# 335 single moves in the planned engine queues of a two-layer attention and mixer kernel

## The chip, the cores and the metric

The kernel runs on one core of a Trainium2 chip. Such a core has five engines with a queue each: TensorE (PE in the profile; PEld is its weight load), VectorE (DVE), ScalarE (ACT), GpSimd (POOL) and SyncE (SP), which here issues DMA transfers. An engine works through its own queue strictly in the order in which it was written; engines wait for one another by semaphores. Matmul results land in eight PSUM banks, called b0 to b7 here. The metric is the time of one execution in microseconds (us); the time before is the median of three runs.

## The reference

Two layers, each an attention block and a mixer block, on x of 2048 rows (S) and 448 columns (D), 16 heads of 28 columns, F = 1792. The layer norms have no weights.

```python
def _A_ref(x, wqkv, wo):
    qkv = (x @ wqkv).reshape(B, S, 3, H, Dh)          # transposed to q, k, v by head
    scores = einsum("bhqd,bhkd->bhqk", q, k) * Dh ** -0.5
    p = softmax(scores, axis=-1)
    o = einsum("bhqk,bhkd->bhqd", p, v)
    return o.transpose(0, 2, 1, 3).reshape(B, S, D) @ wo

def _B_ref(x, w1, w2, w3, w4):
    h = gelu(layernorm(x) @ w1)
    # the four quarters of h's columns shifted by 1, -1, 2, -2 rows: g0 .. g3
    hs = concatenate([g0, g1, g2, g3], axis=-1) @ w2
    x1 = x + hs
    return x1 + gelu(layernorm(x1) @ w3) @ w4

x = x + _A_ref(layernorm(x));  x = x + _B_ref(layernorm(x))     # layer 1
x = x + _A_ref(layernorm(x));  x = x + _B_ref(layernorm(x))     # layer 2
```

## The kernel before, in words

All 16 heads of both layers' scores are cut into blocks of 128 keys by 512 queries (or the same number of elements in two key tiles by 256 queries). Four blocks, one for each head of a group, belong together, because a head has 28 columns and takes 32 of TensorE's 128 rows. The blocks form one stream through both layers. It is fed by the layer norm, the transposed normalized rows xT, and the projections to q, k and v; each finished chunk of rows passes on through wo and the mixer block while the stream runs on with other blocks.

*The exponentials.* ScalarE takes units of three blocks and of two blocks in turn (`unit_banks`, L1526): a wide unit in banks b0 to b2 (1536 columns) and a narrow one in b3 and b4 (1024 columns). `t_scores` (L1621) plans the score matmuls of a unit (`score_ops`, issued at L1500), `t_exp` (L1723) the exponential that reads them (L1738) and writes into PT, a ring of 15 slots; so unit u can't start before the PV matmuls of unit u − 6 have read their slots. As there are two sets of banks, the scores of the unit after next can only be written when an exponential has ended. Some blocks are kept from ScalarE: `d_first` (L1582) and the four steps of `d_chain` (L1609, L1611, L1613, L1616) compute them on VectorE with a polynomial.

*PV.* `t_pv` (L1750) plans probabilities times values: `mm` (L896) issues one matmul of 32 output rows per head, and the four heads of a group sit in the four column tiles of bank b5 and run together, as one round. At the end of a segment (a chunk of queries, a group of heads, a range of keys) `t_norm` (L1805) copies bank b5 out (L1819), and at a query chunk's end sends the denominators through rT (L1833, L1834) and rscr (L1836) and loads their broadcast into fb (L1841), all by DMAs on SP's queue; L1845 multiplies and writes otn.

*The rest of TensorE's work.* `mm4` (L898, issued at L905) splits a matmul of 128 output rows into the four column tiles. It serves the projections (wk_pad, wq_pad, wv), the statistics for q and k (sq with astat or astatq), wo (wo_pad with otn), w1 and w2, w3 (kT with w in the profile's names, because the transposed rows lie in a part of kT) and w4 (w with h2T). These go through banks b6 and b7. Evacuations on VectorE are L1252 and L1297 (k, q), L1326 (q), L1342 (v), L1902 (wo added to x_res), L2163 (w3) and L2201 (w4 added to x_res); L1238 squares q and k on POOL. Wide GELUs run on ScalarE over 7168 columns (L2185). The last chunk's groups are evacuated with the GELU itself, and its w4 goes out through `t_store` (L2213: L2216 on VectorE, L2220 on SP). Transposed rows come by a transposing DMA (`load_xT`, L1223, and `tr_dma`, L1115, both on SP) or by TensorE (`tr_pe`, L1118). `keep_pe_busy` (L403) puts filler matmuls on the identity (L2231) where TensorE would stand still for long.

*What sets the order.* Generators hand over operations; the list scheduler `Sched` (L275 on) runs them in planned time with planned durations and appends each operation to its engine's queue in `Plan` (L47 on). Nothing of this is decided on the chip. Each operation has a number, its position in the order of registration, over all engines. `Plan.add` (L160) finds the dependencies from what was registered before: the last writers of what is read, the last readers and writers of what is written. `finalize` (L194) makes semaphore waits of them and leaves out the waits already implied; `emit` (L245) writes each queue.

After the scheduler is done, `rearranged` (L120) may edit the queues. It takes operation a out of its engine's queue and puts it right behind operation b, for each pair (a, b) of `MOVES`, and then registers all operations again, in the order that `WEAVE` gives: one letter for each operation, t for TensorE, s for ScalarE, v for VectorE, g for GpSimd, d for SP, each taking the next operation of that engine's edited queue. Dependencies and waits are derived anew from this. If an operation would then read another writer's data, it raises an error.

```python
for (a, b) in moves:
    q = nxt[b]
    nxt[b], prv[a], nxt[a] = a, b, q
    if q is not None:
        prv[q] = a
```

In the kernel before both tables are empty (L19, L20) and `rearranged` isn't called (L2278).

Of the kernel before, what the change touches and what calls it, by code (L numbers as in the profile page):

```python
# [15 lines left out]
ENGS = ("pe", "act", "dve", "pool", "sp")  # L16


MOVES = ()  # L19
WEAVE = ()  # L20


class _Op:
# [646 lines left out]
def build_kernel(nc, A_x, A_wqkv, A_wo, B_x, B_w1, B_w2, B_w3, B_w4, out, n_layers=2):  # L670
# [85 lines left out]
    with st:  # L756
# [1520 lines left out]

        if WEAVE:  # L2278
            P = P.rearranged(MOVES, "".join(WEAVE))
        P.finalize(nc, st)  # L2280
# [55 lines left out]
```

## Time and profile before

| | before |
|---|---|
| median of 3 runs | 1029.74 us |
| lowest and highest | 1028.24, 1032.38 us |
| the profiled execution | 1028.64 us |
| its span | 1026.9 us |
| mean granted TensorE clock | 0.998 |

The profile is of one execution. Its span reaches from the first to the last recorded instruction; 1.74 us of the execution's time lie around it. "PT<-ps" names what an instruction writes and reads (buffer numbers left out), "128x1536" is partitions by elements, "x375" counts instructions. In square brackets stands how long the engine sat idle directly before, and what ended that. Records of neighbouring instructions on one engine can overlap, so short waits don't show as idle time. Rows of PE count its instructions; four matmuls of the four column tiles that run together count as four.

### The profile page before, as it was taken

The page shows a single profiled execution, that of the slowest core. Times are in us where ns is not written, and L with a number is a line of the kernel's source. Part 1 is how long each engine was busy: PE and PEld are TensorE (multiplying, and loading weights), DVE is VectorE, ACT ScalarE, POOL GpSimd, SP SyncE. Part 2 cuts the span into 40 slices and gives each one's busy share as a digit, 9 for nine tenths or more (in the row PEclk, how much of TensorE's full clock was granted, in tenths as well). Part 3 has the DMA queues.
Part 4 walks back from the last instruction along what each step waited for, and adds up shares of the span by engine and source line. Part 5 has one row for each costly group of instructions (what it writes and reads, how often), then busy time and mean ns, then how long its engine had stood idle before and what let it go on. Part 6 is the DMA issues. An engine that isn't in the chain of part 4 may idle for free.

```text
span 1026.9 us, 35814 instructions
## 1 busy us (share of the span) xinstructions
PE 973.9 (95%) x16107; PEld 410.4 (40%) x16109; DVE 809.6 (79%) x1572; ACT 983.0 (96%) x894; POOL 294.7 (29%) x462
## 2 busy tenths in 40 slices
PE   8999999999999999999999999999999999999998
PEld 3332444443333254343433443443434433444565
DVE  8876999999988958976867868697788588866651
ACT  7999999999999999999999999999999999999942
POOL 3312021430353006352435112012633130532230
PEclk9999999999999999999999999999999999999999
DMA  4633232220321013122241124424311020121101
GB/s 125 150 108 112 73 107 76 57 39 23 75 61 28 12 37 89 30 48 33 52 106 38 33 59 145 139 59 106 64 30 34 13 71 18 29 56 32 26 12 34
DMA packets 99393, 62.55 MB, mean 61 GB/s; under 512 B 68712, under 2 KB 88552, under 8 KB 99240
## 3 DMA queue, kind: packets, MB, share of 16 engines
q1 hardware_dynamic: 99240, 60.27, 23.3%
q8 instruction: 126, 2.06, 0.9%
q14 instruction: 27, 0.22, 0.1%
HBM read 28.16 MB, written 16.76 MB: 44 GB/s over the span
## 4 chain that ended last, share of the span: by engine, by line
ACT 67%; PE 28%; DVE 3%; DMA 1%; issue 1%; SPq 1%; DVEq 0%; ACTq 0%
ACT PT L1738 61%; PE ps L905 16%; PE ps L1500 6%; PE ps L896 5%; ACT h2T L2185 2%; ACT fb L2004 1%; DMA fb<-rscr 1%; ACT L2185 0%; DMA PT<-in_A_wqkv_dram 0%; DMA obf<-in_A_x_dram 0%; DVE yd L1582 0%; ACT sq L1235 0%; ACT hT L1986 0%; DVE PD L1616 0%; SPq L1223 0%
## 5 line engine op out<-in xcount | busy, mean ns | idle before, releaser
L1738 ACT ACTIVATE PT<-ps 128x1024 bf16<-128x1024 f32 (+1 forms) x782 | 887.7, 1318 | 5.8 <-PE ps L1500 3.6
L1500 PE MATMUL ps<-qT,kT 32*128 32x512 bf16 (+1 forms) x2304 | 270.1, 335 | 23.5 <-ACT PT L1738 17.3
L896 PE MATMUL ps<-PT,vaug 128*32 128x512 bf16 (+1 forms) x2420 | 247.2, 341 | 0.4
L905 PE MATMUL ps<-xT,w 128*32 128x512 bf16 (+3 forms) x2656 | 183.9, 344 | 4.3 <-DVE h2T L2163 2.4
L1500 PEld LDWEIGHTS ps<-qT,kT 32*128 32x128 bf16 x2304 | 69.9, 91 | 254.5 <-ACT PT L1738 222.0
L2231 PE MATMUL ps<-ident 128*32 128x256 bf16 x3348 | 146.0, 277 | 1.6 <-POOL ident L990 1.5
L896 PEld LDWEIGHTS ps<-PT,vaug 128*32 128x32 bf16 x2420 | 74.0, 95 | 89.6 <-issue 73.1
L2231 PEld LDWEIGHTS ps<-ident 128*32 128x32 bf16 x3348 | 95.4, 98 | 27.2 <-issue 11.6
L1845 POOL TENSOR_TENSOR otn<-ub,fb 128x512 bf16<-128x512 f32 (+1 forms) x31 | 36.6, 1180 | 208.7 <-DMA fb<-rscr 199.0
L905 PEld LDWEIGHTS ps<-xT,w 128*32 128x32 bf16 (+1 forms) x2656 | 70.0, 95 | 58.2 <-issue 26.7
L1582 DVE TENSOR_SCALAR yd<-ps 128x512 int32<-128x512 f32 x109 | 74.5, 685 | 19.1 <-PE ps L1500 18.3
L905 PE MATMUL ps<-w,h2T 128*32 128x448 bf16 x1120 | 76.8, 359 | 5.9 <-ACT h2T L2185 5.8
L1609 DVE SCALAR_TENSOR_TENSOR fb<-yd 128x512 f32<-128x512 uint16 x109 | 78.4, 724 | 0.5
L1611 DVE SCALAR_TENSOR_TENSOR fb<-fb,yd 128x512 f32<-128x512 f32 x109 | 77.2, 710 | 0.7
L1616 DVE SCALAR_TENSOR_TENSOR PD<-yd,PD 128x512 int16<-128x512 int16 x109 | 76.4, 702 | 1.6
L2163 DVE CAST h2T<-ps 128x512 bf16<-128x512 f32 (+1 forms) x70 | 44.5, 636 | 17.6 <-PE ps L905 16.5
L1238 POOL TENSOR_TENSOR sq<-qT 128x512 bf16<-128x512 bf16 x24 | 28.4, 1188 | 92.0 <-DVE qT L1297 89.1
L1238 POOL TENSOR_TENSOR sq<-kT 128x512 bf16<-128x512 bf16 (+2 forms) x32 | 30.3, 948 | 84.4 <-DVE kT L1252 81.3
L1613 DVE TENSOR_SCALAR PD<-fb 128x512 bf16<-128x512 f32 x109 | 49.7, 458 | 1.0
L905 PE MATMUL ps<-xT,wk_pad 128*32 128x512 bf16 (+2 forms) x576 | 47.7, 359 | 0.5 <-DVE vaug L1342 0.2
L905 PE MATMUL ps<-xT,wq_pad 128*32 128x512 bf16 x512 | 43.4, 382 | 0.6 <-issue 0.5
L905 PEld LDWEIGHTS ps<-w,h2T 128*32 128x32 bf16 x1120 | 30.3, 97 | 31.2 <-issue 10.2
(189 smaller groups left out, 1213.4 us busy)
## 6 DMA issues: line engine op xcount, KB each, us to landing
uscr<-ub SPq DMA_DIRECT2D x28, 256.0 KB
ub<-uscr SPq DMA_DIRECT2D x28, 256.0 KB, 7.0
fb<-rscr SPq DMA_DIRECT2D x24, 256.0 KB
xnd<-xn SPq DMA_DIRECT2D x28, 128.0 KB, 2.4
xd<-x_res SPq DMA_DIRECT2D x16, 224.0 KB, 2.2
x_res<-xd SPq DMA_DIRECT2D x16, 224.0 KB, 3.9
w<-in_B_w_dram SPq DMA_DIRECT2D x5, 448.0 KB, 7.5
obf<-in_A_x_dram SPq DMA_DIRECT2D x16, 112.0 KB
```

The source lines that it names most:

```text
L896: return lambda e: e.matmul(out=out, lhsT=lhsT, rhs=rhs, start=start, stop=stop, **kw)
L905: r.append(e.matmul(out=out[c:c + w, :], lhsT=lhsT[:, c:c + w], rhs=rhs, start=start, stop=stop, tile_position=(0, c)))
L1238: return both("sq", 0.15 + NW * 0.0018, 0.07 + NW * 0.00104, lambda e: e.tensor_tensor(out=sq[:, si, 0:NW], in0=src, in1=src, op=ALU.mult) ...
L1500: yield op("pe", (0.005 + NW * 0.00042) / nc_, lambda e, i=i, kc=kc, j=j, g=g, qt=qt, a=a, NW=NW, bank=bank: e.matmul(out=ps[:, bank, i * ...
L1582: yield op("dve", c_ps(512), lambda e: e.tensor_scalar(out=y, in0=ps[:, bi(bank), :], scalar1=SCALE * L2E * FS, scalar2=-126.0 * FS, op0=A ...
L1609: yield op(D_[0][0], D_[0][1], lambda e: e.scalar_tensor_tensor(out=q, in0=lo, scalar=E2 / E3 * FS, in1=lo, op0=ALU.add, op1=ALU.mult), re ...
L1611: yield op(D_[1][0], D_[1][1], lambda e: e.scalar_tensor_tensor(out=q, in0=q, scalar=E1 / E3 * FS * FS, in1=lo, op0=ALU.add, op1=ALU.mult) ...
L1613: yield op(D_[2][0], D_[2][1], lambda e: e.tensor_scalar(out=pdt, in0=q, scalar1=E3 / FS ** 3, scalar2=E0, op0=ALU.mult, op1=ALU.add), rea ...
L1616: yield op(D_[3][0], D_[3][1], lambda e: e.scalar_tensor_tensor(out=pdt.bitcast(I16), in0=hi, scalar=128.0, in1=pdt.bitcast(I16), op0=ALU. ...
L1738: yield op("act", 0.069 + n * w * 0.000833, lambda e, bk=bk, s0=s0, n=n, w=w: e.activation(out=PT[:, s0:s0 + n, 0:w], in_=ps[:, bk[0]:bk[0 ...
L2163: ev = op("dve", c_ps(m * NW), lambda e, hr=hr, pv=pv: e.tensor_copy(out=hr, in_=pv), reads=[("ps", bi(b))], writes=hk, touch=[b])
L2231: return [e.matmul(out=ps[32 * c:32 * c + 32, bi(b), 0:256].rearrange("p (a n) -> p a n", n=128), lhsT=ident[:, 32 * c:32 * c + 32], rhs=i ...
```

## The change

`MOVES` gets 335 pairs and `WEAVE` 104 strings of 11,186 letters in all. Nothing else in the source changes; every line below the tables stands 146 further down. By engine, 247 of the moved operations are TensorE's, 56 VectorE's, 17 GpSimd's, 9 SyncE's and 6 ScalarE's. 82 go to a later place, 253 to an earlier one or follow a moved neighbour (chains such as (564, 575), (565, 564) keep a group together behind its first). The letters come to 7914 t, 880 s, 1572 v, 458 g and 362 d, which is the number of operations of each engine before. None of the moves goes into the first 24 us of the profile; the last ones are in the stretch after the last exponential.

```diff
-MOVES = ()
-WEAVE = ()
+MOVES = (
+    (241, 247), (243, 241), (274, 285), (276, 274), (555, 550), (572, 568), (574, 572), (564, 575), (565, 564),
...
+    (759, 758), (856, 850), (857, 856), (858, 857), (930, 935), (931, 930), (937, 931), (966, 951), (975, 987),
...
+    (3339, 3343), (3787, 3779), (3788, 3787), (3900, 3883), (3901, 3900), (3891, 3895), (3917, 3933), (3919, 3917),
...
+    (5286, 5292), (5360, 5379), (5361, 5360), (5362, 5361), (5363, 5362), (5406, 5399), (5407, 5406), (5409, 5407),
+    (5410, 5409), (5457, 5491), (5746, 5683), (5700, 5717), (5701, 5700), (5745, 5739), (5820, 5836), (5822, 5820),
...
+    (9616, 9627), (9680, 9672), (9681, 9680), (9682, 9681), (9684, 9682), (9697, 9689), (9699, 9697), (9700, 9699),
...
+    (4904, 4882), (5515, 5505), (5488, 5515), (5593, 5607), (5678, 5657), (5912, 5878), (5951, 5905), (6131, 6120),
...
+    (1299, 1282), (4296, 4191), (4869, 4832), (7465, 7418), (7510, 7578), (8305, 8253), (11184, 11171),
+)
+WEAVE = (
+    "vdvvvvsgdvgvvdtgtvgdtvtgdtsgtgvdvtvttdvtvvtdttvtvdgtgtdvtvtdtstvvtdgsvtttdtsgtttttstttsvttttvstttttgtvttstttvt",
...
+)
```

Operations that the prediction names: 241 and 243 are the two scores of 24.14 us in the profile before; 3900 and 3901 the two w4 groups of 381.49, 3891 the wo group of 380.29; 756, 758 and 759 the three wv groups of 74.62; 5745 and 5746 the w4 group of 518.91 and the w3 group of 519.10; 9616 the first xT,w group of 887.06; 7465 the transposing load issued at 690.86; 5678 the addition (L2201) of 512.33.

101 lines of the change are left out of this document (added), and 34 rows, old and new, of the table MOVES.

## The prediction

> **What bounds the kernel now.** I read the page's busy shares first, then its chain by engine, then the stretch between the first and last exponential (exp) in the view of windows (after length and colon: busy us of PE, PEld, DVE, ACT and POOL, granted clock, DMA share, GB/s), the groups by shape, the chain in time, and at last the queues around each wait.
>
> ```profile
> span 1026.9 us, 35814 instructions
> PE 973.9 (95%) x16107; PEld 410.4 (40%) x16109; DVE 809.6 (79%) x1572; ACT 983.0 (96%) x894; POOL 294.7 (29%) x462
> ACT 67%; PE 28%; DVE 3%; DMA 1%; issue 1%; SPq 1%; DVEq 0%; ACTq 0%
> L1738 ACT ACTIVATE PT<-ps x782: 821/1277/1767, 16.2 to 971.9; 128x1536 bf16<-128x1536 f32 x190, 128x1024 bf16<-128x1024 f32 x6
> 16.21:972.90 956.69, 909.52 (x14715) 370.64 (x14719) 778.50 (x1482) 950.62 (x846) 281.18 (x424) 1.00 0.24 61
> L1738 ACT ACTIVATE PT<-ps 128x1536 bf16<-128x1536 f32 x375 | 577.0, 1539 | 5.7 <-PE ps L1500 3.6 <-PE ps L896 0.8
> L1738 ACT ACTIVATE PT<-ps 128x1024 bf16<-128x1024 f32 x406 | 447.8, 1115 | 0.1
> 114.05 89.09 ACT PT L1738 x79
> 999.42 23.83 PE ps L905 x532
> ```
>
> ScalarE is busy 950.62 of the 956.69 us from the first exp to the end of the last: 6.07 us of idle time shows. That understates the waits. The chain's unbroken run of 79 exps took 89.09 us, 2.255 us for a pair of a wide and a narrow one (39.5 pairs), while the records of such a pair last 1539 + 1115 = 2654 ns: neighbours overlap by 0.2 us each, and a wait shorter than that overlap isn't shown at all. By the spacing of the ends of all 782 exps against that cadence, the waits add up to about 10.7 us: four of 0.8 to 1.2 us, 17 of 0.15 to 0.5 us, the rest smaller. This is all that any order of the same work can win in this stretch, because the moves change neither the exps nor the GELUs. The 16.2 us ahead of it hold none of the moves. In the 55 us behind, the chain is matmul without a gap (532 in 23.83 us at its end), and the same matmuls are left.
>
> **The change part by part.** Of the 335 moves 247 are on PE, 56 on VectorE (DVE), 17 on GpSimd (POOL), 9 on SP and 6 on ScalarE. Every engine keeps its operations. The semaphore waits go from 4689 to 4665. So nothing is removed and nothing added; a move is worth what it takes off one of those waits. What comes directly ahead of 158 of the exps changes.
>
> *Rounds ahead of scores.*
>
> ```profile
> 24.14 0.39 PE L1500 MATMUL ps<-qT,kT 32*128 32x512 bf16 x2
> 24.45 0.81 PE L896 MATMUL ps<-PT,vaug 128*32 128x512 bf16 x8
> 24.90 3.71 ACT L1738 ACTIVATE PT<-ps 128x1536 bf16<-128x1536 f32 x3 [0.82 <-PE ps L896]
> 887.06 0.40 PE L905 MATMUL ps<-xT,w 128*32 128x512 bf16 x4 [1.21 <-issue]
> 887.27 0.49 PE L896 MATMUL ps<-PT,vaug 128*32 128x256 bf16 x9
> 887.51 0.90 PE L905 MATMUL ps<-xT,w 128*32 128x512 bf16 x12
> 888.34 0.39 PE L1500 MATMUL ps<-qT,kT 32*128 32x256 bf16 x6
> 888.78 6.88 ACT L1738 ACTIVATE PT<-ps 128x1536 bf16<-128x1536 f32 x6 [1.13 <-PE ps L1500]
> ```
>
> The exp at 24.90 waits for PV matmuls (L896) that free its PT slots. Two scores (moves 241 and 243) now go behind them: the PVs start at 24.14 in place of 24.45, a gain of 0.31. The scores come later by the first rounds, and are needed only when that wide exp is over, after 26.2. At 888.78 the exp waits for scores behind sixteen xT,w matmuls, and PE stands still for 1.21 us ahead of these. The nine PVs that ran among them are now put into that idle time. Four matmuls on the four column tiles run together as one round; by the tail's 532 in 23.83 us a round of 448 columns takes 0.179 us, so one of 256 columns 0.10. Nine PVs are three rounds: 0.31. The remaining 0.9 of this stall is the late xT and stays.
>
> *Filling holes in PE's queue.*
>
> ```profile
> 379.57 0.40 PE L896 MATMUL ps<-PT,vaug 128*32 128x256 bf16 x7
> 380.29 0.37 PE L905 MATMUL ps<-wo_pad,otn 128*32 128x448 bf16 x4 [0.32 <-DVE x_res L1902]
> 381.49 0.55 PE L905 MATMUL ps<-w,h2T 128*32 128x448 bf16 x8
> 73.89 0.37 PE L905 MATMUL ps<-wv,xT 128*32 128x448 bf16 x4
> 74.39 0.61 PE L896 MATMUL ps<-PT,vaug 128*32 128x512 bf16 x7
> 518.91 0.36 PE L905 MATMUL ps<-w,h2T 128*32 128x448 bf16 x4
> 519.10 0.28 PE L905 MATMUL ps<-kT,w 128*32 128x256 bf16 x4
> 519.21 0.38 PE L896 MATMUL ps<-PT,vaug 128*32 128x512 bf16 x1
> ```
>
> Two w4 groups (x8 at 381.49) go in among the PVs ahead of the 0.32 hole and no longer stand ahead of the next scores: up to 0.32; I take 0.30. The three wv groups behind the waiting PVs of 74.39 go ahead of them, into the gap 74.26 to 74.39: 0.13, taken as 0.15 for the shorter tail. The w3 group of 519.10 leaves its window and the w4 group of 518.91 goes one place up, so that the PV of 519.21, which waits for its block, needs nothing but its wait behind it: 0.11 (to 519.21) at least, up to 0.30, taken 0.20. About twenty smaller places of the same kind (a group less, or a hole filled, ahead of an exp with under 0.1 us to spare, each 0.05 to 0.24 by the same rounds of 0.10 or 0.18) come to 1.1. Where groups went, other windows get one or two rounds more; four of those have next to no slack: minus 0.4.
>
> *SP's queue.* Move 7465 takes the transposing load out of the way of a normalization.
>
> ```profile
> 690.86 2.69 SPq L1223 DMA_TRANSPOSE xT<-xnd  x1
> 693.59 0.55 SPq L1841 DMA_DIRECT2D fb<-rscr  x1
> 700.81 0.69 DVE L1845 TENSOR_TENSOR otn<-ub,fb 128x512 bf16<-128x512 f32 x1 [2.25 <-DMA fb<-rscr]
> 701.42 0.74 DVE L1297 TENSOR_SCALAR wk_pad<-ps,bc 128x512 bf16<-128x512 f32 x1
> 702.31 0.40 PE L905 MATMUL ps<-sq,astatq 128*32 128x512 bf16 x4 [0.94 <-DVE wk_pad L1297]
> 703.72 8.45 ACT L1738 ACTIVATE PT<-ps 128x1536 bf16<-128x1536 f32 x7 [0.66 <-PE ps L1500]
> ```
>
> The issue of 2.69 us stood ahead of the load of fb; VectorE waited 2.25 us for fb, its q evacuation behind was late, PE waited 0.94 for that, and the exp 0.66. With the transposes issued earlier, fb lands about 1.75 us earlier, still 0.5 us of VectorE's 2.25 remain, and PE's 0.94 is gone: the exp's 0.66 goes, and with what the overlap hides I take 0.70. The four DMA instructions of a normalization (L1833, L1836, L1802, L1841) keep their order among each other; the other eight SP moves go past weight loads that wait for nothing.
>
> *VectorE, POOL, ScalarE moves.* These 79 mostly bring an evacuation or a POOL product forward by one to three places. No row gives their price: above, it can't exceed the waits that PE's and SP's moves leave alone and that an evacuation could end (some 3 us, out of the rest of 10.7); below, there is the cost worked out under the VectorE rival. I take 0.9, near the lower middle, since most stalls rest on PE's order and only a few on an evacuation.
>
> *The tail.* Three w3 groups are postponed, transposes come earlier, and the last two banks swap their order. PE has no gap there to fill: 0.
>
> Sum: 0.31 + 0.31 + 0.30 + 0.15 + 0.20 + 1.1 − 0.4 + 0.70 + 0.9 = 3.6 us. The profiled execution took 1028.64 us (1.74 around its span of 1026.9); less 3.6, 1025.0. The runs' median, 1029.74, lies 1.1 above the profiled run; I leave that out of the centre and in the range. Half a per cent, what a measurement can tell from no change, is 5.1 us: faster means under 1024.6, slower over 1034.9, and the forecast sits on the first of these.
>
> **The throttle.**
>
> ```profile
> 903.21 2.25 PE L905 MATMUL ps<-w,h2T 128*32 128x448 bf16 x32 [1.96 <-ACT h2T L2185]
> 901.25:903.21 1.96, 0.00 (x1) 0.00 (x1) 0.00 (x0) 1.96 (x2) 0.72 (x1) 1.00 0.07 26
> 904.21:907.62 3.41, 3.41 (x44) 1.48 (x40) 0.78 (x3) 3.38 (x3) 0.00 (x0) 0.50 0.02 5
> 367.60:369.56 1.96, 0.00 (x1) 0.01 (x2) 0.00 (x0) 1.94 (x2) 0.00 (x0) 1.00 0.00 0
> 906.27 2.37 ACT L1738 ACTIVATE PT<-ps 128x1536 bf16<-128x1536 f32 x2
> 909.61 3.71 ACT L1738 ACTIVATE PT<-ps 128x1536 bf16<-128x1536 f32 x3 [0.97 <-PE ps L1500]
> ```
>
> After PE stood still 1.96 us for the wide GELU the granted clock was 0.50 for 3.41 us, and the exp at 909.61 came 0.97 late. The same 1.96 us at 367.60 were followed by no such stretch, so it depends on more than the gap. A PE that is packed more densely ahead of a GELU stands still longer before it; each such case costs about 1 us. I count none, and put it into the range.
> [...]
>
> **The rivals.**
> *More goes than I can place* (chance 0.22). Exps with little lead are released by chains that cross engines; moves for which I found no wait may each take a part of the 10.7 us. If the stalls not touched by name (0.97 at 909.61 and some 2 us of evacuation waits) are all that is left, 7.7 go: 1021. For it: 335 moves are spread over the whole stretch. Against: I found a wait behind about 30 only.
> *Waits reappear* (0.15). A stall that one exp loses comes back at the next, as when the xT transfer or fb is late by itself: then only 0 to 1 us is won and the kernel gives 1029. For it: the remaining 0.9 at 888.78. Against: an exp that starts earlier lets the next bank go earlier too, and no DMA but those two stands at a large wait.
> *VectorE held up by its own queue* (0.13, slower).
>
> ```profile
> 510.41 0.68 DVE L1611 SCALAR_TENSOR_TENSOR fb<-fb,yd 128x512 f32<-128x512 f32 x1
> 511.93 0.36 PE L905 MATMUL ps<-w,h2T 128*32 128x448 bf16 x2
> 512.33 0.62 DVE L2201 TENSOR_TENSOR x_res<-x_res,ps 128x448 f32<-128x448 f32 x1 [1.23 <-PE ps L905]
> ```
>
> Move 5678 puts the addition of 512.33 ahead of L1611 of 510.41, but its matmuls end at 512.29 (511.93 + 0.36): L1611 and the exp block done on VectorE behind it would start at 512.95, 2.5 us later. At seven more places an operation is put 0.4 to 1.4 us ahead of its input as the old order had it. If PE's moves don't bring these inputs forward, eight such delays of 1.8 us on average (mean of the waits 1.0 and the operation itself 0.6 to 0.7), of which 0.5 is covered, and all of it on the way to exps, make 8 × 1.3 = 10.4: 1028.64 − 3.6 + 10.4 = 1035.4. It decides where the blocks on VectorE have under 1.3 us to spare. Against: the operation behind is mostly a step of a block whose PV comes microseconds later, and PE's order was changed at those same places.
> That the change doesn't do what it says is excluded: the queues differ as the table has it, and each operation still reads the data of the same writers.
>
> **How the numbers follow.** Forecast 1025.0 at 0.50 (split by the edge 1024.6: 0.23 faster, 0.27 same); more 0.22, all faster; reappear 0.15, all same; VectorE 0.13, of which 0.11 over 1034.9. Faster 0.45, same 0.27 + 0.15 + 0.02 = 0.44, slower 0.11. The range goes from 1019 (the rival that wins more, with a spread of 2) to 1033 (reappearing waits, 1029, with the median's offset of 1.1 and three throttled stretches); the forecast's own is 1022 to 1028.
>
> **What would show it.** Right: the idle time before wide exps falls from 5.7 to about 3; the waits at 24.90, 382.42 and 703.72 are gone; the one at 888.78 shows 0.8 in place of 1.13; fb lands before VectorE has waited 1 us; the tail's length from the last exp to the end is the same. Wrong: exps that start on time now wait (new bracketed idles behind L1738), or VectorE shows waits of 1 us at L2201, L1902, L1819 with its blocks late, or several stretches of clock 0.50, or the stretch of exps shortens by more than 6 us, which would mean waits that the records hide.

## The result and the profile after

| | before | after |
|---|---|---|
| median of 17 runs each | 1028.24 us | 1025.12 us |
| lowest and highest | 1025.51, 1032.38 us | 1023.95, 1028.69 us |
| ratio of the runs | 1 | 0.9972, 95% interval 0.9961 to 0.9982 |
| the profiled execution, its span | 1028.64, 1026.9 us | 1025.07, 1023.4 us |

The medians lie 3.1 us apart; the forecast was 3.6 off the profiled execution, and 1025.0 us in all. The change is under half a per cent, which the prediction calls the same; it gave that 0.44 and faster 0.45. The page of the profile after, its windows from the first to the last exponential (exp) and its ScalarE groups by shape, as they were shown of before; all lines of the code stand 146 further down (L1738 is L1884):

```profile
span 1023.4 us, 35818 instructions
PE 969.9 (95%) x16109; PEld 408.7 (40%) x16109; DVE 813.1 (79%) x1572; ACT 981.0 (96%) x894; POOL 291.4 (28%) x462
15.96:969.55 953.59, 905.43 (x14708) 368.82 (x14710) 782.22 (x1482) 949.07 (x845) 277.94 (x424) 1.00 0.24 61
L1884 ACT ACTIVATE PT<-ps 128x1536 bf16<-128x1536 f32 x375 | 582.2, 1553 | 2.8 <-PE ps L1646 1.6 <-PE ps L1042 0.3
L1884 ACT ACTIVATE PT<-ps 128x1024 bf16<-128x1024 f32 x406 | 453.0, 1130 | 0.7 <-PE ps L1646 0.6
```

The last exp of before ended at 972.72, so its window of 956.69 us in the prediction reached 0.18 too far. The two spans differ by 3.57 us: 0.25 lie ahead of the first exp, where no move stands; 2.92 lie between the first and the last exp (956.50 and 953.58 us); 0.40 lie in the tail behind (54.20 and 53.80 us). The idle time ahead of wide exps fell from 5.7 to 2.8 us. The tail comes out at 53.8 in all five profiles that hold TensorE's moves and the others' together, at 54.4 with TensorE's alone and at 54.8 with the others' alone, so its 0.4 belongs to the order.

Where? An exp's end in the one trace less the end of the same exp in the other is a line with steps; each step is a wait won or lost at that exp. Here are the places that the prediction names and the largest that stay; pairs that cancel within three exps are left out (such as −0.52 at 420.40 and +0.52 at 423.96):

| exp of before at | step us | what stands there |
|---|---|---|
| 24.90 and the next | −0.51, +0.17 | moves 241, 243 |
| 75.94 | −0.18 | 756, 758, 759 |
| 268.59 | +0.63 | scores behind matmuls that wait for VectorE's x_res, which waits 0.84 us for a load of x |
| 382.42 | −0.31 | 3900, 3901, 3891, and VectorE's 3875 |
| 519.96 | under 0.1 | 5745, 5746 |
| 703.72 | −0.77 | 7465 |
| 755.47 | +0.88 | a tanh on ScalarE waits for VectorE |
| 867.09 | +0.81 | scores behind matmuls that wait for VectorE |
| 888.78 | −0.41 | 9616 |
| 909.61 | −1.08 | a stretch of half clock (0.50 for 3.41 us) in the profile before, none there after |

The timeline of ScalarE after, at five of these places (start, us, then what; in brackets the idle time before and what ended it):

```profile
24.14 3.88 ACT L1884 ACTIVATE PT<-ps 128x1536 bf16<-128x1536 f32 x3 [0.31 <-PE ps L1042]
378.83 6.98 ACT L1884 ACTIVATE PT<-ps 128x1536 bf16<-128x1536 f32 x6
697.88 9.40 ACT L1884 ACTIVATE PT<-ps 128x1024 bf16<-128x1024 f32 x8
887.03 6.88 ACT L1884 ACTIVATE PT<-ps 128x1536 bf16<-128x1536 f32 x6 [0.72 <-PE ps L1646]
904.51 3.71 ACT L1884 ACTIVATE PT<-ps 128x1536 bf16<-128x1536 f32 x3
```

At 24.14 the wait is 0.31 in place of 0.82, at 887.03 0.72 in place of 1.13; at 382.42 and 703.72 of before the exps now run on without one. The last row is the place of 909.61: no wait either. For 703.72, the queues of SyncE and VectorE after:

```profile
685.58 1.95 SPq L1369 DMA_TRANSPOSE xT<-xnd  x1
687.71 0.50 SPq L1982 DMA_DIRECT2D rscr<-rT  x1
690.21 0.56 SPq L1987 DMA_DIRECT2D fb<-rscr  x1
696.83 0.68 DVE L1991 TENSOR_TENSOR otn<-ub,fb 128x512 bf16<-128x512 f32 x1
```

The transposing load now stands ahead of rscr, in time that SyncE spent waiting for the reciprocals; fb is issued at 690.21 in place of 693.59, and VectorE's product doesn't wait.

The two large losses show on VectorE, whose rows here run past the two rows of GpSimd (POOL):

```profile
750.99 1.77 DVE L1755 SCALAR_TENSOR_TENSOR fb<-yd 128x512 f32<-128x512 uint16 x1
752.68 0.68 DVE L2149 SCALAR_TENSOR_TENSOR fb<-fb,hT 112x512 f32<-112x512 f32 x1
861.39 1.76 DVE L1757 SCALAR_TENSOR_TENSOR fb<-fb,yd 128x512 f32<-128x512 f32 x1
863.41 0.68 DVE L2309 CAST h2T<-ps 128x512 bf16<-128x512 f32 x1
...
750.91 1.30 POOL L1991 TENSOR_TENSOR otn<-ub,fb 128x512 bf16<-128x512 f32 x1 [8.38 <-DMA fb<-rscr]
861.32 1.29 POOL L1991 TENSOR_TENSOR otn<-ub,fb 128x512 bf16<-128x512 f32 x1 [24.22 <-DMA fb<-rscr]
...
753.39 0.63 ACT L2150 ACTIVATE fb<-fb 112x512 f32<-112x512 f32 x1 [0.77 <-DVE fb L2149]
864.14 0.40 PE L1051 MATMUL ps<-xT,w 128*32 128x512 bf16 x4 [0.80 <-DVE h2T L2309]
865.87 4.62 ACT L1884 ACTIVATE PT<-ps 128x1536 bf16<-128x1536 f32 x4 [0.71 <-PE ps L1646]
```

Two operations that mostly take 0.68 us took 1.77 and 1.76 us, each started within 0.1 us behind a GpSimd product of normalization (otn). What stands behind them on VectorE came 1.08 us late: the second step of a tanh GELU (L2149), for which ScalarE waited 0.77, and a w3 evacuation (L2309), for which TensorE waited 0.80 and the exp 0.71. In the prediction neither of these is a term. The trace before had the same kind of row, behind which no exp waited; the product beside it began at 150.34:

```profile
150.62 1.76 DVE L1609 SCALAR_TENSOR_TENSOR fb<-yd 128x512 f32<-128x512 uint16 x1
```

### The profile page after: what moved, and what is told of

Same layout as the page of the kernel before. It is cut to its first block, busy times and chain, and to the rows that moved or that the text cites. A ratio compares the mean times of both kernels' runs of the same rounds, so it can differ in the third digit from the quotient of the medians.

```text
span 1023.4 us, 35818 instructions
## 1 busy us (share of the span) xinstructions
PE 969.9 (95%) x16109; PEld 408.7 (40%) x16109; DVE 813.1 (79%) x1572; ACT 981.0 (96%) x894; POOL 291.4 (28%) x462
## 4 chain that ended last, share of the span: by engine, by line
ACT 71%; PE 23%; DVE 3%; DMA 1%; issue 1%; SPq 0%; DVEq 0%; ACTq 0%
ACT PT L1884 65%; PE ps L1051 13%; PE ps L1646 5%; PE ps L1042 4%; ACT h2T L2331 2%; ACT fb L2150 1%; PE ps L2377 1%; ACT L1884 1%; DVE h2T L2309 0%; ACT hT L2132 0%; DMA rT<-ub 0%; ACT L2331 0%; DMA PT<-in_A_wqkv_dram 0%; DMA obf<-in_A_x_dram 0%; DMA rscr<-rT 0%
## 5 line engine op out<-in xcount | busy, mean ns | idle before, releaser
L1884 ACT ACTIVATE PT<-ps 128x1024 bf16<-128x1024 f32 (+1 forms) x782 | 887.4, 1332 | 3.5 <-PE ps L1646 2.2
L1051 PE MATMUL ps<-xT,w 128*32 128x512 bf16 (+4 forms) x2656 | 178.1, 344 | 4.2 <-DVE h2T L2309 3.0
L1755 DVE SCALAR_TENSOR_TENSOR fb<-yd 128x512 f32<-128x512 uint16 x109 | 79.0, 728 | 0.7
L1757 DVE SCALAR_TENSOR_TENSOR fb<-fb,yd 128x512 f32<-128x512 f32 x109 | 78.3, 721 | 0.7
L2309 DVE CAST h2T<-ps 128x512 bf16<-128x512 f32 (+1 forms) x70 | 44.4, 635 | 16.0 <-PE ps L1051 14.9
L1646 PE MATMUL ps<-wk_pad,kT 32*128 32x512 bf16 x256 | 39.6, 384 | 4.5 <-ACT PT L1884 4.0
```

The lines of the kernel that those rows point to most:

```text
L1051: r.append(e.matmul(out=out[c:c + w, :], lhsT=lhsT[:, c:c + w], rhs=rhs, start=start, stop=stop, tile_position=(0, c)))
L1646: yield op("pe", (0.005 + NW * 0.00042) / nc_, lambda e, i=i, kc=kc, j=j, g=g, qt=qt, a=a, NW=NW, bank=bank: e.matmul(out=ps[:, bank, i * ...
L1755: yield op(D_[0][0], D_[0][1], lambda e: e.scalar_tensor_tensor(out=q, in0=lo, scalar=E2 / E3 * FS, in1=lo, op0=ALU.add, op1=ALU.mult), re ...
L1757: yield op(D_[1][0], D_[1][1], lambda e: e.scalar_tensor_tensor(out=q, in0=q, scalar=E1 / E3 * FS * FS, in1=lo, op0=ALU.add, op1=ALU.mult) ...
L1884: yield op("act", 0.069 + n * w * 0.000833, lambda e, bk=bk, s0=s0, n=n, w=w: e.activation(out=PT[:, s0:s0 + n, 0:w], in_=ps[:, bk[0]:bk[0 ...
L2309: ev = op("dve", c_ps(m * NW), lambda e, hr=hr, pv=pv: e.tensor_copy(out=hr, in_=pv), reads=[("ps", bi(b))], writes=hk, touch=[b])
```

## The experiments

Each kernel holds a part of the table `MOVES`; the letters of `WEAVE` register the edited queues again, by operation number as far as the data allow. The time of each stands beside runs of the kernel before on the same chip.

**No moves.**

```diff
-    (241, 247), (243, 241), (274, 285), (276, 274), (555, 550), (572, 568), (574, 572), (564, 575), (565, 564),
...
-    (1299, 1282), (4296, 4191), (4869, 4832), (7465, 7418), (7510, 7578), (8305, 8253), (11184, 11171),
```

> No moves at all; only the letters that register the old order again, so the queues and waits are those of the kernel before. Both theories expect the time of before (ratio 1.000, within 0.001). The profile is a second look at the same program: stalls that come from the order should come back in place and size (24.9: 0.93 end to end; 703.7: 0.77; 888.8: 1.24). Theory 'the 1.08 us that the changed kernel won at the exp of 909.61 is the throttle's luck': the half-clock stretch after the wide GELU near 903 is missing or elsewhere here in some looks. Rival 'the stall at 909.61 belongs to the old order': it is back with about 1.0 us.

1029.0 us, ratio 1.0008 (0.9996 to 1.002). The stalls of the order came back (no step of over 0.15 us at 24.9, 382.4 and 703.7). The one of 909.61 didn't: the exp there came 1.08 earlier than in the profile before. Other places were late instead:

```profile
369.47 4.52 PE L1009 MATMUL ps<-w,h2T 128*32 128x448 bf16 x56 [1.96 <-ACT h2T L2289]
370.10:373.50 3.40, 3.40 (x44) 1.59 (x40) 0.00 (x0) 2.98 (x3) 0.00 (x0) 0.50 0.17 63
374.36 2.37 ACT L1842 ACTIVATE PT<-ps 128x1536 bf16<-128x1536 f32 x2 [1.26 <-PE ps L1604]
```

The 56 matmuls behind the wide GELU took 2.83 us in the profile before and 4.52 here, at a granted clock of 0.50, and the exp came 1.37 late. Two more stretches of half clock stood near 108, where 0.45 and 0.17 were lost, and near 889, where 1.19 were. So the order before doesn't always lose the 1.08 of 909.61, and it isn't counted as a gain here. (Whether the change makes that loss rarer is taken up in the last section.)

That allows a cleaner comparison: each run lists its mean granted clock, and one stretch of half clock of 3.41 us lowers it by 0.0017 (half of 3.41 in some 1026). So, by this estimate, a run that lists 1.000 had none; the twelve profiled executions agree: 0.995 with three such stretches, 0.996 and 0.997 with two, 0.998 with one, 1.000 with none. Of the 72 runs of the kernel before beside the experiments 27 have a clock of 1.000.

| kernel | runs | mean of all | at clock 1.000: runs, mean |
|---|---|---|---|
| before | 72 | 1028.34 | 27, 1026.97 |
| the changed kernel (17 and 12 of its repeat) | 29 | 1025.62 | 10, 1024.58 |
| the twelve moves | 12 | 1025.67 | 6, 1024.79 |
| without 8107 and 9290 (three times) | 20 | 1024.81 | 6, 1023.38 |

At full clock the order is worth 2.4 us (1026.97 less 1024.58, with a standard error of 0.3), over all runs 2.7.

**TensorE's 247 moves, and the other 88.**

TensorE's pairs stand first in the table; in the one kernel the other 88 are taken out, in the other kernel the 247.

```diff
     (11017, 11016), (11018, 11017), (11177, 11172), (11178, 11177), (11180, 11178), (11181, 11180),
-    (4484, 4523), (5925, 5889), (6339, 6324), (7096, 7213), (8003, 7983), (8678, 8674), (727, 732), (746, 762),
...
-    (8305, 8253), (11184, 11171),
```

```diff
-    (241, 247), (243, 241), (274, 285), (276, 274), (555, 550), (572, 568), (574, 572), (564, 575), (565, 564),
...
-    (11177, 11172), (11178, 11177), (11180, 11178), (11181, 11180),
     (4484, 4523), (5925, 5889), (6339, 6324), (7096, 7213), (8003, 7983), (8678, 8674), (727, 732), (746, 762),
```

> The 247 TensorE moves alone. Theory (the prediction's sum): gains at 24.9, 75.9, 382.4 and 888.8 of 0.3, 0.18, 0.3 and 0.4 as in the changed kernel, nothing at 703.7 (its move is SyncE's), no loss of 0.8 at 753.9 and 865.9 (those come with VectorE's moves): about 2.5 us in all, 1025.7, ratio 0.9975. Rival (the PE moves only pay together with the evacuations that VectorE's moves bring forward): ratio over 0.999.

> The 88 moves of VectorE, GpSimd, SyncE and ScalarE alone. Theory: 0.7 to 0.8 us won at 703.7 by the SyncE move, lost again by two collisions on VectorE of 0.8 to 0.9 each (exps of 753.9 and 865.9), some small gains: ratio 0.999 to 1.001. Prediction's own term: 0.9 + 0.7, ratio 0.9985. Rival of VectorE's held queue: ratio over 1.003, with waits over 1 us at the additions and the exp blocks late.

TensorE's alone: 1027.0 us, ratio 0.9985 (0.9972 to 0.9997); about half of what was expected. The gains at 24.9, 75.9, 382.4 and 888.8 are there (−0.34 net, −0.19, −0.30, −0.40), the losses at 755.5 and 867.1 aren't. Its profile lost 2.5 us elsewhere: 0.44 at a half-clock stretch near 106; 0.66 and 0.28 near 177, where GpSimd's product began 7.16 us behind the issue of fb's load and TensorE waited 1.20 us for it (6.20 us in the kernel with 7465 below, which has the same order up to there and loses nothing); 0.41 at 703.7; 0.50 and 0.24 at 737.7 and 742.2, of which more below. Of its other eleven runs there is no trace. None of the twelve was at clock 1.000, while 13 of the 29 of before beside it were; among the runs under 1.000 the two means, 1029.2 and 1027.0, lie 2.2 apart. The place of 703.7, VectorE, TensorE and ScalarE:

```profile
700.34 0.69 DVE L1977 TENSOR_TENSOR otn<-ub,fb 128x512 bf16<-128x512 f32 x1 [2.65 <-DMA fb<-rscr]
701.84 0.40 PE L1037 MATMUL ps<-sq,astatq 128*32 128x512 bf16 x4 [1.35 <-DVE wk_pad L1429]
703.25 1.45 ACT L1870 ACTIVATE PT<-ps 128x1536 bf16<-128x1536 f32 x1 [1.07 <-PE ps L1632]
```

The waits are 2.65, 1.35 and 1.07 in place of 2.25, 0.94 and 0.66. The chain of transfers wasn't fixed: the exps were 0.88 us earlier than before, and so was SyncE's transfer to rscr (688.81 in place of 689.69). Behind that, the transposing load took 2.92 us to issue in place of 2.69, and fb came 0.18 later after its own issue; together that is the 0.41. In its old place in the queue the issue of this load varies by more than that: 3.13 us with no moves, 3.33 with the seven moves below, none of which is near. So the loss isn't shown to come from TensorE's moves.

The other 88: 1028.08 us, ratio 0.9996 (0.9985 to 1.0007), as expected. The steps at 703.7 (−0.77) and 755.5 (+0.87) cancel. The one at 867.1 isn't there in this profile, so it seems to take TensorE's moves with VectorE's. At 382.4 the exp comes 0.31 earlier here too, without TensorE's three moves; VectorE's 3875 stands there.

**Without 8107 and 9290.**

```diff
-    (8107, 8122), (9290, 9249),
```

> All moves but two of VectorE's: 8107 (second step of a tanh GELU behind the first step of an exp block) and 9290 (third step of an exp block a few places forward). Theory: in the changed kernel each of these let a VectorE operation of 0.68 us run into GpSimd's product otn and take 1.77 us, and the exps of 753.9 and 865.9 came 0.88 and 0.81 late; without them both losses are gone, 1.7 us less than the changed kernel: 1023.4, ratio to before 0.9953, no interval above 0.997. Rival (collisions of this kind are luck of a few tenths of a us and turn up elsewhere): the same time as the changed kernel, ratio 0.997, and other operations of over 1.7 us ahead of an exp.

> The kernel without moves 8107 and 9290 a second time, beside the changed kernel on the same chip, since five runs were too few and its profile's first exp came 0.73 us later than in the changed kernel's. Theory: the exps of 753.9 and 865.9 are again 0.88 and 0.81 earlier than in the changed kernel, and the time at full clock is 1.0 to 1.7 us below it: 1023.3. Rival: the same time, as in the five runs.

> The kernel without moves 8107 and 9290 a third time, for its time beside the other: 14 runs so far have a mean of 1025.1, the changed kernel's 29 one of 1025.7. Theory: 1024.5 to 1025.3, ratio to before 0.996 to 0.997, at full clock below 1024. Rival (the two losses come back in the time by other waits): 1025.7, ratio 0.9975.

1025.28 us in 5 runs, ratio 0.9966 (0.9953 to 0.9978); 1024.81 in 9, 0.9965 (0.9951 to 0.9979); 1023.71 in 6, 0.9957 (0.9941 to 0.9973). In the first two profiles the exps of 755.5 and 867.1 came 0.88 and 0.81 us earlier against the profile after, and in the third neither loss is a step against before, so the two moves are what lost there. The time of the first five runs missed what was expected (1023.4). Their profile's first exp ended 0.73 us later than in the profile after, and up to 268.59, where both kernels have the same order, another 0.8 was lost. Over the 20 runs the time at full clock is 1023.38, 1.2 below the changed kernel, with standard errors of 0.6 and 0.2 (two of its six such runs lie at 1025.3, four at 1022.2 to 1022.7); the mean of all runs, 1024.8 and within what was expected last, is 0.8 below, with an error of 0.4. So the steps show the two losses and their end, and the times go the same way by about twice their error. From the third profile:

```profile
748.95 0.69 DVE L2144 SCALAR_TENSOR_TENSOR fb<-fb,hT 112x512 f32<-112x512 f32 x1
750.62 1.77 DVE L1750 SCALAR_TENSOR_TENSOR fb<-yd 128x512 f32<-128x512 uint16 x1
860.44 0.69 DVE L2304 CAST h2T<-ps 128x512 bf16<-128x512 f32 x1 [0.27 <-PE ps L1046]
861.65 0.68 DVE L1752 SCALAR_TENSOR_TENSOR fb<-fb,yd 128x512 f32<-128x512 f32 x1
...
751.25 0.91 ACT L2145 ACTIVATE fb<-fb 112x512 f32<-112x512 f32 x1
858.42 10.76 ACT L1879 ACTIVATE PT<-ps 128x1536 bf16<-128x1536 f32 x9
```

The first collision is still there, 1.77 us at 750.62 beside a product that began at 750.27, but the step of the tanh now stands ahead of it, and ScalarE doesn't wait. The second is gone: the exp block's step begins at 861.65, after the product of 859.73 (1.27 us) has ended. In the order before, an operation of 1.76 us stood near there too in two profiles (755.63 with no moves, 754.57 with TensorE's alone), but behind the tanh's step, not ahead of it.

**The twelve moves that the prediction names.**

```diff
+MOVES = ((241, 247), (243, 241), (756, 745), (758, 756), (759, 758), (3900, 3883),
+         (3901, 3900), (3891, 3895), (5746, 5683), (5745, 5739), (9616, 9627), (7465, 7418))
```

> Twelve moves alone, those that the prediction gives by number for 24.9 (241, 243), 75.9 (756, 758, 759), 382.4 (3900, 3901, 3891), 519.9 (5745, 5746), 888.8 (9616) and SyncE's 7465 for 703.7. Theory: the steps by which the exps come earlier than before are local and add up: 0.3 + 0.18 + 0.3 + 0.1 + 0.4 + 0.77 = 2.0 us from the first to the last exp, throttled stretches aside, about what all 335 moves won in the same measure (2.92 less the 1.08 of the throttled stretch in the profile of before = 1.84); at full clock about 1024.8, ratio about 0.998. Rival (the many small places carry the gain, as the prediction's 1.1 + 0.9 have it): under 1.2 us, ratio over 0.999.

1025.69 us, ratio 0.9974 (0.9963 to 0.9985): the time of the changed kernel, whose repeat beside it had 0.9974 (0.9962 to 0.9986). At full clock 1024.79, 2.2 under before. The steps at the named places are the same: −0.51 and +0.17, −0.18, −0.31, −0.77, −0.47. Its profile lost 0.31 at 29.07, 0.54 and 1.37 to stretches of half clock near 106 and 369, and 0.46 at 737.7. Twelve moves carry what 335 did. The others seem to win about as much as two of them lose: without 8107 and 9290 the time at full clock is 1.4 below that of the twelve (standard errors 0.6 and 0.3).

**Seven moves on VectorE ahead of their inputs.**

```diff
+MOVES = ((2441, 2434), (3875, 3844), (4393, 4374), (4904, 4882), (5678, 5657), (7298, 7283), (8987, 8969))
```

> Seven of the eight VectorE moves that the prediction's slower rival counts (2441, 3875, 4393, 4904, 5678, 7298, 8987; the eighth hangs on another move), alone, with TensorE's order of before, so that nothing brings their inputs forward. Theory: the operations behind them have room, no exp comes later by more than 0.2 us at any of the seven places, ratio 0.999 to 1.001. Rival: 7 x 1.3 = 9 us, ratio 1.009.

1029.0 us, ratio 1.0003 (0.9989 to 1.0017). VectorE does stand still, and at none of the seven places does an exp come later for it (at 382.4, by 3875, one even comes 0.21 earlier). The place of 5678, VectorE and ScalarE:

```profile
512.64 0.62 DVE L2306 TENSOR_TENSOR x_res<-x_res,ps 128x448 f32<-128x448 f32 x1 [1.78 <-PE ps L1010]
513.17 0.68 DVE L1716 SCALAR_TENSOR_TENSOR fb<-fb,yd 128x512 f32<-128x512 f32 x1
507.58 12.55 ACT L1843 ACTIVATE PT<-ps 128x1024 bf16<-128x1024 f32 x11
```

The addition waits 1.78 us, the step of the exp block starts at 513.17 in place of 510.41, and eleven exps run through without a gap. The block's result is needed later than that.

Two exps elsewhere did come later, by 0.33 at 703.72 and by 0.60 at 737.68, in an order that is unmoved there (the nearest of the seven stands at 674.58). SyncE and TensorE:

```profile
690.92 3.33 SPq L1328 DMA_TRANSPOSE xT<-xnd  x1
737.69 0.83 PE L1010 MATMUL ps<-xT,w 128*32 128x512 bf16 x12 [0.68 <-issue]
```

At 703.72 the transposing load, 0.64 us longer to issue than before, held up fb. At 737.69 TensorE waited for transposed rows: by the semaphore's updates in the trace 15 of the last load's 16 parts had landed at 735.73, the 16th at 737.60. The same late part stands in the profiles of TensorE's moves alone, of the twelve and of TensorE's with 7465, each of which lost 0.46 to 0.60 at 737.7, and in no other. What made it late stays open; it had the same place in the queue in the two profiles without it that hold the old order of SyncE.

**The changed kernel again.**

> The changed kernel itself again. Theory: the two losses at 753.9 and 865.9 come back with 1.77 and 1.76 us of the same VectorE operations, since they belong to the order; the stretch of half clock, if there is one, stands elsewhere. Rival (luck): these two operations take 0.68 us here.

1025.79 us. Both losses are back, +0.85 and +0.81, and so are the two long operations:

```profile
752.21 1.77 DVE L1755 SCALAR_TENSOR_TENSOR fb<-yd 128x512 f32<-128x512 uint16 x1
862.60 1.76 DVE L1757 SCALAR_TENSOR_TENSOR fb<-fb,yd 128x512 f32<-128x512 f32 x1
```

They belong to the order, not to the execution. A stretch of half clock stood behind the wide GELU near 369 this time (+1.37), and the exp of 909.61 was on time.

**TensorE's moves with SyncE's 7465.**

```diff
-    (4484, 4523), (5925, 5889), (6339, 6324), (7096, 7213), (8003, 7983), (8678, 8674), (727, 732), (746, 762),
...
     (7465, 7418),
-    (7510, 7578), (8305, 8253), (11184, 11171),
```

> The 247 TensorE moves and SyncE's move 7465, without the other 87. Theory: TensorE's moves alone lost 0.41 again at the exp of 703.7, since fb's transfer stays behind the transposes whatever the exps do; with 7465 that exp comes 0.77 earlier than in the order before, 1.2 earlier than with TensorE's moves alone, and the two losses at 753.9 and 865.9 are absent. So it should be under the changed kernel by about 1 us (0.88 and 0.81 not lost, some tenths of small gains missing): 1024.7, ratio 0.9965. Rival (VectorE's and GpSimd's moves are worth the 0.9 of the prediction's sum on top): over the changed kernel by about 1 us, ratio 0.998.

1024.55 us in 5 runs, ratio 0.9962 (0.9950 to 0.9974). The exp of 703.7 comes 0.77 earlier, 1.18 better than with TensorE's moves alone, and the two losses are absent. So the steps of TensorE's moves and of 7465 simply add up; that TensorE's need the transfer to be early, as was expected, isn't shown, since the 0.41 came from slower transfers in one execution. At 737.7 and 742.2 it lost 0.60 and 0.23, as TensorE's alone did. The mean of these five runs is 1025.1, 0.5 under the changed kernel's with an error of 0.6, so the other 87 moves add nothing on the whole that these runs could show.

## Why the prediction was right, point by point

**The bound.** It holds in the main that only waits between exps can be won. The tail, which the sum has at 0, gave 0.4 us, so the sum put that too low. Of the signs that the prediction lists, idle time of 2.8, a wait of 0.72 at 888.78 and fb in time are as it says; at 24.90 a wait of 0.31 stayed, and one sign of being wrong is there as well, a new wait of 0.71 ahead of the exp of 865.87.

**The six named places.** Predicted 0.31, 0.31, 0.30, 0.15, 0.20 and 0.70; the steps in the profile after: 0.34, 0.41, 0.31, 0.18, under 0.1 and 0.77. Five of six within 0.1. The miss is 519.96, 0.06 in the profile after and 0.11 with the twelve moves, against a range of 0.11 to 0.30; what else held the scores there stays open. At 888.78 the sizes are loose: 0.20 to 0.59 in the eight profiles with move 9616, and 0.17 and 0.22 in two without it, so part of the 0.41 isn't its doing. At 382.42 the prediction gives the gain to TensorE's groups, and VectorE's moves alone bring it too. The twelve moves alone show that these gains stand by themselves, 2.2 us at full clock.

**The small places (1.1, less 0.4) and the 79 moves of other engines (0.9).** The kernel without the two moves is 1.4 us under the twelve at full clock, against 1.6 by these three terms; with an error of 0.6 this says little, and it holds for all together only. Two of the small places show by themselves: 0.17 at 98.87 and 0.20 at 805.66 are won in each of the seven profiles with TensorE's 247 moves and in none of the others. For the 79 the term itself is mis-sized: VectorE's and GpSimd's moves were given 0.9, and two of them cost 1.69 (0.88 and 0.81). The 88 together, with the 0.77 of 7465 in them, came out at 0.9996. What failed is the lower bound of that term: it took an operation's place on VectorE as the only thing that matters, and not what GpSimd does at that moment. The row for it was there in the trace before, in operations of up to 1.76 us among those of 0.7 (150.62 above), and wasn't read for a price.

**The throttle.** Counted as none, and it wasn't none: 1.08 us of the difference between the two profiles is a stretch of half clock that the profile before had and the profile after hadn't. In the runs it comes and goes with both kernels (45 of 72 and 19 of 29 runs under 1.000). The prediction's fear that a denser TensorE stands still longer ahead of a GELU wasn't borne out: 1.96 us near 368 in all twelve profiles, and near 903 only 1.82 to 1.83 in the seven with TensorE's moves. The predicted 3.6 stands against the 3.1 of the medians and the 2.4 at full clock. Less the two losses (1.7) and with the tail's 0.4 the sum would be 2.3. The forecast of 1025.0 was counted from an execution that held one such stretch. That 1025.12 came so close is in part luck: the sum was too large, and the changed kernel's median run was 0.5 above its full-clock mean.

**The rivals.** *More goes than I can place* didn't happen. *Waits reappear* was given little, and is a part of what was seen, at 268.59 (+0.63, +0.50 in the repeat, no such step in two of the three without 8107 and 9290). VectorE waits there for a load of x: where SyncE took 3.8 us to issue three of these (four profiles), it didn't wait, and where it took 4.30 to 4.66 (the eight others), it waited 0.68 to 1.03. In the profile after, the exps had come 1.58 us earlier up to there, but the load was issued only 1.11 earlier and took 0.16 longer, and a lead of 0.95 was left. Why the issue takes longer in some executions stays open. *VectorE held up by its own queue* is excluded as it was put: VectorE waits up to 1.78 us ahead of exp blocks, and the seven such places cost nothing. VectorE did cost time, but by the collision with GpSimd, and at steps for which ScalarE or TensorE were waiting.

## What to carry to other kernels

Compare the two traces operation by operation and read the steps, rather than the totals: here a dozen steps told more than the times of 29 runs, and of 335 edits twelve were enough for the gain that all of them brought, and two took away 1.7 us. Have several traces of the same order, too: steps at transfers came and went here by up to 0.9 us, and one trace alone would have put them down to the edit. When an order is tuned on queues, look for what runs on the neighbour engine at each place: an operation that something waits for belongs ahead of the one that can collide (1.77 us in place of 0.68 here). And an engine that stands still costs nothing until somebody waits for what is behind it: VectorE's 1.78 us ahead of 512.64 made no exp late.

## What the runs showed of the hardware

A VectorE operation with two inputs in SBUF that starts just behind a product on GpSimd took 1.76 to 1.77 us in place of 0.68 at both places of the changed kernel: L1755 (L1609 before) near 751 us in four profiles, L1757 (L1611) near 862 in two. In the profile after, the products beside them took 1.30 and 1.29 us, and the operations 1.08 more than their 0.68. Evacuations, with their input in PSUM, took 0.69 beside such a product, as the one of 860.44 above, beside the product of 859.73 to 861.00, and those of 838.42 and 864.44 in the trace before. The product can be the longer one as well: in the trace before VectorE's step of 892.00 (L1609) took its 0.68, and the product listed 0.02 us behind it, of 128x256, took 1.26, where three others of that shape took 0.72 to 0.73 (464.59, 876.06, 928.12); at 754.26 and 754.27 they took 0.69 and 1.81, where the product of 864.51, of the same shape, took 1.27. An operation with one SBUF input was hit too, PD<-fb at 160.32 in the trace before, 1.50 us in place of 0.42, 0.16 behind a product of 1.38. What makes one of the two wait for the other isn't shown.

The granted clock changed on a grid in these profiles. In each of the twelve all its changes lie a whole number of 3.413 us apart, the length of the stretch of half clock in the profile before (there they stand 263, 264 and 299 such steps behind the clock's first record, in the profile after 298, with no moves 30, 31, 107, 108, 259 and 260), and where the grid lies against the program differs from execution to execution. Behind the wide GELUs near 368 and 903 TensorE stood still for 1.96 us sixteen times. Nine times the whole 1.96 us lay in one step of the grid, and the next step was at half clock eight times. Seven times a step's end cut it in two, and no half clock followed. Both are in the trace before, near 368 without and near 903 with it:

```profile
364.91:368.32 3.41, 2.69 (x100) 2.34 (x88) 0.85 (x2) 3.41 (x1) 0.00 (x0) 1.00 0.04 7
368.32:371.73 3.41, 2.17 (x48) 1.28 (x52) 0.00 (x0) 3.38 (x3) 0.00 (x0) 1.00 0.16 51
900.80:904.21 3.41, 1.45 (x44) 0.76 (x36) 0.00 (x0) 3.41 (x2) 0.72 (x1) 1.00 0.08 28
904.21:907.62 3.41, 3.41 (x44) 1.48 (x40) 0.78 (x3) 3.38 (x3) 0.00 (x0) 0.50 0.02 5
```

So in these profiles half clock near 368 (six of the twelve, 1.37 us at the exp each time) went with where the grid happened to lie. Near 903 the order may matter: with TensorE's moves TensorE stands still for 1.82 to 1.83 us there, and no half clock followed in those seven profiles, though in four of them it all lay in one step of the grid, with TensorE busy for 1.59 us of it. TensorE's busy time in such a step doesn't settle it: four stretches of half clock elsewhere followed steps in which it was busy for 1.98 to 2.35 us, as here with no moves, while steps with 1.96 us (812.05 to 815.46 in the trace before) and 1.88 (815.06 to 818.48 in the one after) had a clock of 1.00 behind them. What settles it isn't shown.

```profile
103.89:107.31 3.42, 2.23 (x22) 0.60 (x20) 3.31 (x14) 3.42 (x4) 0.00 (x0) 1.00 0.39 134
107.31:110.72 3.41, 3.41 (x39) 1.11 (x40) 3.07 (x5) 3.06 (x4) 1.04 (x1) 0.50 0.22 79
```
